# Buffer addresses, a ring's load order and the engine of some splits, changed together in a Strassen MLP kernel

## The chip, the cores and the metric

The kernel runs on one core of a Trainium2 chip. The metric is the device time of one execution in microseconds (us). All inputs, outputs and sums are float32. TensorE (PE) multiplies, VectorE (DVE), ScalarE (ACT) and GpSimd (POOL) work on tiles of 128 partitions in SBUF, and SyncE (SP) issues the DMAs. Each engine takes its instructions in the order of the program.

## The reference

```python
def reference(q, k, v, moe_w_gate, moe_w_val, moe_w_out, moe2_w_in, moe2_w_out):
    x = attention(q, k, v)                  # 4 x 8 heads, 576 positions of 64, causal by blocks of 64
    x = x.transpose(0, 2, 1, 3).reshape(2304, 512)
    g = x @ moe_w_gate                      # 512 -> 1536
    x = (g * sigmoid(g) * (x @ moe_w_val)) @ moe_w_out          # 1536 -> 512
    h = x @ moe2_w_in                       # 512 -> 2048
    g = np.where(h > 0, h, np.exp(np.minimum(h, 0)) - 1)        # ELU
    return g @ moe2_w_out                   # 2048 -> 512
```

## The kernel before

Each float32 factor is split into a high part (rounded to the type in which TensorE multiplies at full pace) and a low part (the rest), and a product is three matmuls: high by high, high by low, low by high (`mm3`, L213 to L215; written out at L1102 to L1104 and L1211 to L1213). ScalarE makes a high part by a copy, another engine the low part by a subtraction.

The stages follow each other: attention, and gate and value products of the first tokens (to about 345 us); gate and value products of the other tokens with one level of Strassen (to 475 us; tiles `xc`, `bt`, `val`, `xa`); the product with `moe_w_out` (to 603 us; tile `y`); then the second MLP. It runs over three groups of 768 tokens (i = 0, 1, 2) and in each over eight pairs p of 128-wide blocks of the 2048 hidden columns. The products of pair p with `moe2_w_in` are seven Strassen products M1 to M7 (`p3_h`; 42 matmuls of 384 columns, tiles `h`, in group 2 also `o`). ELU is made by ScalarE and VectorE (L1052 to L1056) and split into `gp` buffers (high and low, L1056 and L1058), and in groups 0 and 1 the product with `moe2_w_out` follows (`p3_o`: 36 matmuls of 512 columns a pair, tile `o`, 576 matmuls in all; `gp` is the stationary operand, the parts `OH` and `OL` of the weight the moving one). In group 2 that product is Strassen's too (`p3_o7`, after the last pair, 256 columns each, from about 915 us).

The parts that the change touches:

- **Weights of `moe2_w_out`.** `conv_unit` turns each of its 16 blocks (128 x 512) from the raw words into a work tile of a ring of four (`c`), by ScalarE (L188) and VectorE (L196, L198, L200), makes the high part on ScalarE (L206) and the low part on GpSimd (L210). This happens while group 0 runs, between the pairs (603 to 740 us).
- **Combined weights for group 2.** While group 1 runs, `o_sums` adds high and low parts again (L930, one block of a pair on VectorE and one on GpSimd), combines them (L936), splits the results (L946, L947) and stores them to `o_scr`. Its work tiles are four slots of their own (`co`).
- **The ring of weight slots.** The split Strassen weights lie in DRAM (`w_scr`). `p3_slot` (L1004) loads one product's weights into the next of eight slots of the tile `xa`; a slot is free when the product that used it eight slots ago is done. SyncE takes the loads in the order of the ring.
- **Addresses.** `gp` buffers start 16 words (`YO`, 64 bytes) into the tiles `val` and `bt`. By the addresses of the built program, `bt`, `val`, `oh`, `ol` and `xc` start at multiples of 128 bytes, `xa` 64 bytes beyond one.

The order of the instructions on each engine comes from a list scheduler in the kernel (`Plan`): every task has an engine, an assumed duration, a priority (mostly a due time) and its dependencies. So an edit moves the rows around it too.

```python
ns = [p3_slot(p, o, due3[i, p] + step / 7 * u - 8) for u, o in enumerate((M1, M2, M6, M5, M7, M4, M3))]
g = p3_h(i, p, ns, due3[i, p] - (UY + .5 if i == p == 0 else 0), step)
```

Of the kernel before, what the change touches and what calls it, by code (L numbers as in the profile page):

```python
# [150 lines left out]
def attention_moe_moe_kernel(ctx: ExitStack, tc: tile.TileContext,  # L151
# [50 lines left out]
    def like(c, d):  # L202
        return c.rearrange("p (a b) -> p a b", a=2) if len(d.shape) == 3 else c
# [1 line left out]
    def cv_hi(i):  # L205
        act.copy(cv_units[i][1], like(cv_state[i][1], cv_units[i][1]))  # L206

    def cv_lo(i):
        _, hi, lo = cv_units[i]
        pool.tensor_tensor(lo, like(cv_state.pop(i)[1], lo), hi.bitcast(F32), ALU.subtract)  # L210

    def mm3(dst, wh, wl, xh, xl, start, stop, more=False):
        pe.matmul(dst, wh, xh, start=start, stop=False, skip_group_check=more)  # L213
# [47 lines left out]
    def tr_t():  # L261
# [2 lines left out]


    plan = Plan(dict(raw=3, rawb=2, c=4, rk=2, rq=2, rv=NRV, nm=4, sm=3, pl=NP1, ph=NP1, th=NTH, x=3, sa=1, sb=1, tp=2, gv=2,
                     th1=2, s2=2, st=2, ar=5, ah=NAH, gm=KP, co=4, wo=3, e4=4, gs=12, gt=4, y=6, ys=4, ws=NW, wm=NWM, gp=NP, et=2, hc=4, **{f"ab{p}{r}": 1 for p in range(KP) for r in range(4)}))
    add, nxt = plan.add, plan.nxt


# [22 lines left out]
    def conv_unit(i, prio, after=(), whole=False, first=()):  # L293
        cn[i], rn[i] = nxt("c"), nxt("raw" if i < 2 * K1 else "rawb")
        r, c, w = ("raw" if i < 2 * K1 else "rawb", rn[i], 0), ("c", cn[i], 0), ("w", i, 0)
        add("SP", 450, lambda: cv_dma(i), prio, writes=[r], after=first, data=1900 if i == 1 else 1430)
        add("ACT", 575, lambda: cv_a(i), prio, [r], [c])
        for p, ns in enumerate((340, 650, 650) if i < 2 * K1 else (340, 602, 602)):
            if p == 0 and CVP and 4 <= i < 2 * K1 and i % 2 >= 2 - CVP:
                add("POOL", 900, lambda: cv_b(i, 0, pool), prio, [r, c], [c])  # L300
                continue
            add("DVE", ns, lambda p=p: cv_b(i, p), prio, [r, c], [c], data=-1000 if p == 2 and i >= 2 * K1 else 0.0, both=i < 2 * K1)
        if whole:
            return
        add("ACT", 520, lambda: cv_hi(i), prio, [c], [w], after)
        add("POOL", 1250 if i < 2 * K1 else 1400, lambda: cv_lo(i), prio, [c, w], [w])


    heads = lambda t, n: t.rearrange("p (h d) -> p h d", d=n)
# [354 lines left out]
    ar_b, ys_b, abt, pa_t = [], [], [], []  # L664
    OSEQ = M1, M6, M2, M7, M5, M4, M3 = range(7)
    PSEQ = M1, M2, M6, M5, M7, M4, M3
    OH, OL, ws, wm, gp, yqt = {}, {}, {}, {}, {}, {}

    def yq(r):
        return yqt[r].rearrange("p k t -> p (k t)")  # L670
# [247 lines left out]
        strassen_weights(part, ck, whole, prio, split)  # L918

    def o_sums(p, prio):  # L920
        n = [nxt("co") for _ in range(2)]
        part = lambda r, c: pa_t[0][:, 512 * (n[c] % 4) + 256 * r:512 * (n[c] % 4) + 256 * r + 256]
        ck = lambda r, c: ("co", n[c], r)
        plan.group = "o0"
        for x in range(2):
            add("SP", 450, lambda x=x: sp.dma_start(out=o_scr[p][0][:, 256 * x:256 * x + 256], in_=(OH, OL)[x][2 * p][:, 0:256].bitcast(F32)), prio, [("w", unit["o", 2 * p], 0)], [("oscr", p, (M1, x))], data=400)
        for c in range(2):
            def build(c=c):
                f, w = 2 * p + c, pa_t[0][:, 512 * (n[c] % 4):512 * (n[c] % 4) + 512]
                (pool if c else dve).tensor_tensor(w, OH[f].bitcast(F32), OL[f].bitcast(F32), ALU.add)  # L930

            add(*(("POOL", 1400) if c else ("DVE", 690)), build, prio, [("w", unit["o", 2 * p + c], 0)], [ck(0, c), ck(1, c)], [("p3", 0, 0), ("yscr", NG - 1, 2), ("od", (p - 1) % HP, 0)], data=-2000)
        plan.group = None

        def comb(d, x, y, op):
            add("DVE", 420, lambda: dve.tensor_tensor(part(*d), part(*x), part(*y), op), prio, [ck(*x), ck(*y)], [ck(*d)])  # L936

        def split(o, x):
            n = nxt("wo")
            hk, lk = ("wo", n, 0), ("wo", n, 1)  # L940

# [15 lines left out]
        comb(a11, a12, a11, ALU.subtract)  # L957
        split(M3, a11)
# [47 lines left out]
        add("SP", 450, load, prio, [("wscr", p, o)], [("ws", n, 0), ("ws", n, 1)], [("p2", 0, 0)], data=700)  # L1006
        return n

    def p3_h(i, p, ns, due, step):
        q = i * HP + p  # L1010
        m1, u2, u3 = range(3) if i >= S7 else (nxt("hc") for _ in range(3))
        hck = lambda n: ("hc", n, 0)
# [54 lines left out]
        X, Y = q % 2, 1 - q % 2  # L1067
        Z = 2 if three else Y
        for u, (o, b, new) in enumerate(((M1, X, True), (M2, Z, True), (M6, X, False), (M5, Y, True), (M7, X, False), (M4, X, False), (M3, Y, False))):
            for k in range(2):  # L1070
                def mm(u=u, o=o, k=k, b=b, new=new):
                    w, ks, ys = ws[ns[u]], slice(128 * k, 128 * k + 128), slice(HT * k, HT * k + HT)
                    mm3(bank(b), w[:, 0, ks], w[:, 1, ks], yop(o, 0)[:, ys], yop(o, 1)[:, ys], new and k == 0, k == 1, True)

                add("PE", 525, mm, due + u * step / 7 + .01 * k, [("ws", ns[u], 0), ("ws", ns[u], 1), ("yo", o, 0)],
                    [hbk(b)] + ([("hd", i, 0)] if p == HP // 2 and u == 0 and k else [("he", i, 0)] if p == HP - 1 and u == 0 and k else []))
# [50 lines left out]
    def p3_o7(i, due):  # L1127
# [12 lines left out]
        def split(o, p, r, u):  # L1140
            v = nxt("gp")
            hk, lk = ("gp", v, 0), ("gp", v, 1)
            g = lambda k: gp[v % NP][k]
            pr = due - HSTEP * (HP - p) + 10 if u == 0 else by(u, p)
            eng, en, ns = (pool, "POOL", 1100) if u == 0 or p in PLO else (dve, "DVE", 557)
            add("ACT", 412, lambda: act.copy(g(0), gb(p, r)), pr, [gk(p, r)], [hk])
            add(en, ns, lambda: eng.tensor_tensor(g(1), gb(p, r), g(0).bitcast(F32), ALU.subtract), pr, [gk(p, r), hk], [lk])
            return v

# [38 lines left out]
        for u, o in enumerate(seq):  # L1188
# [12 lines left out]
            tail = last and o == M4  # L1201
            for n, (p, j) in enumerate([(p, j) for j in range(3) for p in range(HP)] if tail else [(p, j) for p in range(HP) for j in range(3)]):
                def mm(o=o, p=p, j=j, b=b, new=new, v=vs[p], n=ns.get(p)):
                    h, l = (t[:, 128 * j:128 * j + 128] for t in gp[v % NP])
                    if o in OST:
                        wh, wl = ws[n][:, 0], ws[n][:, 1]
                    else:
                        cs = slice(256 * (o == M4), 256 * (o == M4) + 256)
                        wh, wl = OH[2 * p + 1][:, cs], OL[2 * p + 1][:, cs]
                    d = region(b, (j,))  # L1210
                    pe.matmul(d, h, wh, start=new and p == 0 and j != 1, stop=False, skip_group_check=True)  # L1211
                    pe.matmul(d, h, wl, start=False, stop=False, skip_group_check=True)
                    pe.matmul(d, l, wh, start=False, stop=p == HP - 1, skip_group_check=True)  # L1213
# [385 lines left out]
```

## Time and profile before

| what | value |
|---|---|
| median of 3 runs (lowest, highest) | 982.23 us (982.12, 982.48) |
| the profiled execution | 982.16 us |
| its span in the trace | 980.3 us (1.86 us lie outside) |
| TensorE busy in the span | 965.4 us, 98% |
| VectorE, ScalarE, GpSimd busy | 791.6, 647.7, 244.8 us |
| granted TensorE clock | 1.00, in every slice |

Busy time of TensorE is the union of instructions whose ends are modelled and overlap: a matmul is shown about 0.2 us longer than its distance to the next one. So the pace is read from start to start, and a wait is the extra distance between two starts.

### The profile page before, as it was taken

How to read it: one execution, taken by the hardware profiler on the slowest of the kernel's cores; microseconds unless marked ns; L12 is line 12 of the kernel's file. 1: busy time of each engine (PE TensorE's matmuls, PEld its weight loads, DVE VectorE, ACT ScalarE, POOL GpSimd, SP SyncE). 2: the span in 40 equal slices, each digit the busy share in tenths (PEclk: the TensorE clock that was granted, in tenths of full speed). 3: DMA queues.
4: the chain of work that ended last, by engine and by line, in shares of the span. 5: the costliest groups of instructions: out<-in, count | busy, mean ns of one | idle time of the engine just before them, and what ended most of it. 6: DMA issues, size and time to landing. Idle time of an engine off the chain costs nothing.

```text
span 980.3 us, 18628 instructions
## 1 busy us (share of the span) xinstructions
PE 965.4 (98%) x6266; PEld 871.5 (89%) x6266; DVE 791.6 (81%) x1614; ACT 647.7 (66%) x1521; POOL 244.8 (25%) x243
## 2 busy tenths in 40 slices
PE   9999999999999999999999999999999999999998
PEld 8789988888889978887999999889888888899998
DVE  7999677666867795789999996987977687977993
ACT  6998678888987644556765665665665455666653
POOL 3333442332324623000001101223302323311131
PEclk9999999999999999999999999999999999999999
DMA  6767465566576679774764705787646676596663
GB/s 224 235 201 220 138 193 175 203 214 193 180 247 228 216 262 351 221 254 154 239 194 125 252 17 151 246 275 271 179 123 216 188 240 191 177 295 222 229 208 116
DMA packets 116463, 202.56 MB, mean 207 GB/s; under 512 B 12304, under 2 KB 51216, under 8 KB 116368
## 3 DMA queue, kind: packets, MB, share of 16 engines
q1 hardware_dynamic: 116224, 201.24, 63.5%
q8 instruction: 50, 0.82, 0.4%
q14 instruction: 45, 0.37, 0.1%
q10 hardware_dynamic: 144, 0.13, 0.0%
HBM read 141.56 MB, written 59.77 MB: 205 GB/s over the span
## 4 chain that ended last, share of the span: by engine, by line
PE 86%; DVE 7%; DMA 2%; ACT 2%; issue 1%; POOL 1%; SPq 0%; ACTq 0%; DVEq 0%; POOLq 0%
PE gv L213 7%; PE gv L215 7%; PE gv L214 7%; PE y L213 6%; PE y L214 6%; PE y L215 6%; PE tp L506 5%; PE h L213 4%; PE sa L480 4%; PE h L215 4%; PE h L214 4%; PE o L1104 3%; PE o L1103 3%; PE o L1102 3%; PE tp L601 2%; PE o L1211 2%
## 5 line engine op out<-in xcount | busy, mean ns | idle before, releaser
L213 PE MATMUL gv<-xa,bt 128*128 128x256 f32 x240 | 72.7, 303 | 0.6 <-DVE tt L655 0.6
L213 PE MATMUL gv<-xa,val 128*128 128x256 f32 x240 | 71.9, 300 | 0.0
L213 PE MATMUL h<-val,xa 128*128 128x384 f32 x204 | 69.0, 338 | 0.8 <-ACT xq L1065 0.6
L215 PE MATMUL h<-val,xa 128*128 128x384 f32 x204 | 68.6, 336 | 0.0
L214 PE MATMUL h<-val,xa 128*128 128x384 f32 x204 | 68.4, 335 | 0.0
L606 ACT COPY th<-tp 128x512 f32<-128x512 f32 x96 | 53.7, 593 | 21.7 <-PE tp L602 21.5
L215 PE MATMUL gv<-xa,val 128*128 128x256 f32 x240 | 67.1, 280 | 0.5 <-POOL val L210 0.5
L214 PE MATMUL gv<-xa,bt 128*128 128x256 f32 x240 | 67.0, 279 | 0.0
L215 PE MATMUL gv<-xa,bt 128*128 128x256 f32 x240 | 67.0, 279 | 0.0
L214 PE MATMUL gv<-xa,val 128*128 128x256 f32 x240 | 67.0, 279 | 0.0
L210 POOL TENSOR_TENSOR bt<-c,bt 128x512 fp32r<-128x512 f32 x20 | 30.9, 1547 | 125.7 <-ACT bt L206 65.7
L1313 POOL TENSOR_TENSOR wy<-c,wy 128x256 fp32r<-128x256 f32 x48 | 39.5, 836 | 87.9 <-ACT wy L1312 87.8
L761 ACT ACTIVATE val<-a 128x384 fp32r<-128x384 f32 x80 | 40.8, 524 | 25.3 <-PE y L215 22.7
L915 POOL TENSOR_TENSOR val<-c,val 128x256 fp32r<-128x256 f32 x14 | 12.7, 912 | 174.5 <-ACT val L914 174.4
L506 PE MATMUL tp<-th,rv 128*64 128x256 f32 (+1 forms) x512 | 55.5, 359 | 0.0
L915 POOL TENSOR_TENSOR wy<-c,wy 128x256 fp32r<-128x256 f32 x42 | 32.6, 791 | 86.6 <-ACT wy L914 61.0
L1054 DVE SCALAR_TENSOR_TENSOR xq<-xq,xq 128x384 f32<-128x384 f32 x64 | 38.9, 611 | 14.4 <-ACT xq L1053 14.0
L650 DVE SCALAR_TENSOR_TENSOR tt<-tt,gv 128x256 f32<-128x256 f32 x60 | 25.0, 417 | 31.3 <-ACT tt L646 30.9
L506 PEld LDWEIGHTS tp<-th,rv 128*64 128x64 f32 x512 | 33.9, 136 | 18.2 <-ACT c L188 0.3
L480 PE MATMUL sa<-rk,rq 64*128 64x320 f32 (+2 forms) x192 | 49.9, 393 | 0.0
L480 PE MATMUL sb<-rk,rq 64*128 64x320 f32 (+2 forms) x192 | 49.9, 393 | 0.0
L213 PEld LDWEIGHTS gv<-xa,bt 128*128 128x128 f32 x240 | 45.3, 189 | 4.8 <-issue 2.9
(425 smaller groups left out, 3677.3 us busy)
## 6 DMA issues: line engine op xcount, KB each, us to landing
xa<-w_scr SPq DMA_DIRECT2D x168, 256.0 KB, 3.3
a<-a_scr SPq DMA_DIRECT2D x67, 192.0 KB, 3.5
g_scr<-wy SPq DMA_DIRECT2D x48, 256.0 KB, 2.9
xa<-g_scr SPq DMA_DIRECT2D x48, 256.0 KB, 4.3
w_scr<-wy SPq DMA_DIRECT2D x42, 256.0 KB, 4.4
xa<-o_scr SPq DMA_DIRECT2D x40, 256.0 KB, 3.3
raw<-in_w2i_dram SPq DMA_DIRECT2D x16, 512.0 KB, 4.4
raw<-in_w2o_dram SPq DMA_DIRECT2D x16, 512.0 KB, 4.0
```

Of the source, the lines that this page charges most:

```text
L210: pool.tensor_tensor(lo, like(cv_state.pop(i)[1], lo), hi.bitcast(F32), ALU.subtract)
L213: pe.matmul(dst, wh, xh, start=start, stop=False, skip_group_check=more)
L214: pe.matmul(dst, wh, xl, start=False, stop=False, skip_group_check=more)
L215: pe.matmul(dst, wl, xh, start=False, stop=stop, skip_group_check=more)
L480: pe.matmul(sc[2 * p + j][:, at:at + w], raw["rq"][us, QW * p + 128 * q:QW * p + 128 * q + 128], raw["rk"][us, ext * p + o:ext * p + o + w ...
L506: pe.matmul(st["pv"][64 * j:64 * j + 64, QW * p + o:QW * p + QW], raw["rv"][:, p * (nf + 1) + c, 64 * j:64 * j + 64], x[:, at:at + QW - o] ...
L606: act.copy(out["th", c // 2], st["tr", c])
L761: add("ACT", 412, lambda: act.activation(t(0), ab(p, r, g), ACTF.Copy, scale=0.5), by(u, p), [abk(p, r)], [hk], ([("xcd", o, 0) for o in ( ...
L915: add("POOL", 1000, lambda: pool.tensor_tensor(t()[:, 256:512], part(*x), t()[:, 0:256].bitcast(F32), ALU.subtract), prio, [ck(*x), hk] + ...
L1054: add("DVE", 575, lambda: dve.scalar_tensor_tensor(t(), e(), 1.0, t(), ALU.add, ALU.mult), PMP, [tk, ek], [tk])
L1102: pe.matmul(d, h, OH[f][:, cs], start=(p == 0 and u < 2), stop=False, skip_group_check=True)
L1313: add("POOL", 800, lambda: pool.tensor_tensor(t()[:, 256:512], part(*x), t()[:, 0:256].bitcast(F32), ALU.subtract), prio, [ck(*x), hk] + w ...
```

## The change: what it does

1. `gp` buffers are at offset 0 of their tiles for groups 0 and 1; group 2 uses buffers at the old offset (`gp7`), and the first of its splits wait for the last matmul of `p3_o`.
2. In group 2, from pair 1 on, the slots of the next pair's M1 and M2 are taken between this pair's M7 and M4.
3. `o_sums` takes its work tiles from the ring `c`, builds both sums on VectorE, and waits for `p3_o` of group 0 once instead of pair by pair.
4. The low parts of `moe2_w_out` are made by VectorE.

```diff
-    def cv_lo(i):
+    def cv_lo(i, eng=pool):
         _, hi, lo = cv_units[i]
-        pool.tensor_tensor(lo, like(cv_state.pop(i)[1], lo), hi.bitcast(F32), ALU.subtract)
+        eng.tensor_tensor(lo, like(cv_state.pop(i)[1], lo), hi.bitcast(F32), ALU.subtract)
...
-        add("POOL", 1250 if i < 2 * K1 else 1400, lambda: cv_lo(i), prio, [c, w], [w])
+        if i < unit["o", 0]:
+            add("POOL", 1250 if i < 2 * K1 else 1400, lambda: cv_lo(i), prio, [c, w], [w])
+        else:
+            add("DVE", 690, lambda: cv_lo(i, dve), prio, [c, w], [w])
...
     def o_sums(p, prio):
-        n = [nxt("co") for _ in range(2)]
+        n, full = [nxt("c") for _ in range(2)], {}
...
-                (pool if c else dve).tensor_tensor(w, OH[f].bitcast(F32), OL[f].bitcast(F32), ALU.add)
+                full[c] = w
+                dve.tensor_tensor(w, OH[f].bitcast(F32), OL[f].bitcast(F32), ALU.add)
...
+            if u == 5:
+                if i >= S7 and 0 < p < HP - 1:
+                    need(p + 1, (0, 1))
+                need(p, (5, 6))
+            n = slots[i, p, u]
...
-            g = lambda k: gp[v % NP][k]
+            g, old = (lambda k: gp7[v % NP][k]), [("od", HP - 1, 0)] * (i == S7 and u == 0)
...
-            gp[k] = [vals_t[0][:, YO + 2 * HT * k + HT * x:YO + 2 * HT * k + HT * x + HT] for x in range(2)] if k < 4 else [flat[2 * k + 8 + x][:, YO:YO + HT] for x in range(2)]
+            gp[k], gp7[k] = ([vals_t[0][:, a + 2 * HT * k + HT * x:a + 2 * HT * k + HT * x + HT] for x in range(2)] if k < 4 else [flat[2 * k + 8 + x][:, a:a + HT] for x in range(2)] for a in (0, YO))
...
-            ns = [p3_slot(p, o, due3[i, p] + step / 7 * u - 8) for u, o in enumerate((M1, M2, M6, M5, M7, M4, M3))]
-            g = p3_h(i, p, ns, due3[i, p] - (UY + .5 if i == p == 0 else 0), step)
+            need = lambda x, us, i=i, step=step: [slots.setdefault((i, x, u), p3_slot(x, HSEQ[u], due3[i, x] + step / 7 * u - 8)) for u in us if (i, x, u) not in slots]
+            need(p, range(5 if i >= S7 and p else 7))
+            g = p3_h(i, p, need, due3[i, p] - (UY + .5 if i == p == 0 else 0), step)
```

**The ring's loads.** SyncE's loads for pairs 2 to 7 of group 2, before (`w_scr_85` holds the weights of pair 2, `w_scr_90` of pair 7):

```order
L1004 DMA xa<-w_scr_85 128x512 x3
L1004 DMA xa<-w_scr_86 128x512 x7
L1004 DMA xa<-w_scr_87 128x512 x7
L1004 DMA xa<-w_scr_88 128x512 x7
L1004 DMA xa<-w_scr_89 128x512 x7
L1004 DMA xa<-w_scr_90 128x512 x7
L967 DMA xa<-o_scr_75 128x512
```

The same place after the change:

```order
L1008 DMA xa<-w_scr_86 128x512 x2
L1008 DMA xa<-w_scr_85 128x512 x2
L1008 DMA xa<-w_scr_86 128x512 x3
L1008 DMA xa<-w_scr_87 128x512 x2
L1008 DMA xa<-w_scr_86 128x512 x2
L1008 DMA xa<-w_scr_87 128x512 x3
L1008 DMA xa<-w_scr_88 128x512 x2
L1008 DMA xa<-w_scr_87 128x512 x2
```

Two loads of each next pair now stand ahead of the last two of a pair. TensorE takes the products in such an interleaved order already before.

**The low parts.** GpSimd's rows in group 0 before; `L210` are the low parts of `moe2_w_out`, `L930` a sum of `o_sums`:

```order
L210 TENSOR_TENSOR bt_116<-c,bt_115 128x512
L210 TENSOR_TENSOR ol_7307<-c,oh_7306 128x512
L210 TENSOR_TENSOR bt_118<-c,bt_117 128x512
L210 TENSOR_TENSOR ol_7309<-c,oh_7308 128x512
L210 TENSOR_TENSOR bt_120<-c,bt_119 128x512
L210 TENSOR_TENSOR ol_7311<-c,oh_7310 128x512
L930 TENSOR_TENSOR a<-bt_105,bt_106 128x512
```

None of these stands on GpSimd after the change. VectorE's rows before, at the end of that stretch (about 697 to 706 us; L1061 adds a product to a kept one and frees the PSUM bank for which TensorE waits):

```order
L198 SCALAR_TENSOR_TENSOR c<-raw_101,c 128x512
L1061 TENSOR_TENSOR xq_140<-h_5993,xq_140 128x384
L200 SCALAR_TENSOR_TENSOR c<-raw_101,c 128x512
L849 TENSOR_TENSOR raw_101<-tt,raw_100 128x768
L1054 SCALAR_TENSOR_TENSOR xq_142<-xq_143,xq_142 128x384
L1055 SCALAR_TENSOR_TENSOR xq_142<-xq_142,xq_140 128x384
L1054 SCALAR_TENSOR_TENSOR xq_142<-xq_143,xq_142 128x384
L1061 TENSOR_TENSOR xq_141<-h_5993,xq_141 128x384
```

VectorE's rows after, at the same place (L1061 is now L1067, L1054 and L1055 are L1060 and L1061, L849 is L852):

```order
L210 TENSOR_TENSOR bt_120<-c,bt_119 128x512
L1067 TENSOR_TENSOR xq_140<-h_5993,xq_140 128x384
L196 TENSOR_SCALAR c<-c 128x512
L198 SCALAR_TENSOR_TENSOR c<-raw_101,c 128x512
L200 SCALAR_TENSOR_TENSOR c<-raw_101,c 128x512
L1060 SCALAR_TENSOR_TENSOR xq_142<-xq_143,xq_142 128x384
L1067 TENSOR_TENSOR xq_141<-h_5993,xq_141 128x384
L1061 SCALAR_TENSOR_TENSOR xq_142<-xq_142,xq_140 128x384
L1060 SCALAR_TENSOR_TENSOR xq_142<-xq_143,xq_142 128x384
L210 TENSOR_TENSOR ol_7311<-c,oh_7310 128x512
```

The low parts stand between ELU and the conversions, and the combination of L849 comes later than the addition (L1067) that frees the bank.

## Rows read from the trace of the kernel before

**Rows 1.** Page, part 1, TensorE: busy time, share of the span, instructions.

```profile
PE 965.4 (98%) x6266; PEld 871.5 (89%) x6266; DVE 791.6 (81%) x1614; ACT 647.7 (66%) x1521; POOL 244.8 (25%) x243
```

**Rows 2.** Windows by stage: length, busy time (count) of each engine, clock, DMA.

```profile
475.00:603.00 128.00, 128.00 (x740) 128.00 (x739) 117.77 (x236) 77.64 (x159) 6.39 (x7) 1.00 0.46 151
603.00:740.00 137.00, 133.88 (x665) 118.95 (x664) 118.60 (x199) 86.92 (x182) 33.55 (x24) 1.00 0.71 222
740.00:862.00 122.00, 121.84 (x606) 108.86 (x605) 95.56 (x165) 68.11 (x153) 38.57 (x39) 1.00 0.64 203
862.00:916.00 54.00, 51.36 (x287) 49.00 (x287) 41.90 (x77) 36.35 (x82) 6.93 (x7) 1.00 0.78 252
```

**Rows 3.** TensorE's waits, whole span: us in total, times, longest.

```profile
PE h L213 <- DVE xq L1061: 2.5, 2, 1.5
PE h L213 <- DMA xa<-w_scr: 2.4, 3, 1.3
```

**Rows 4.** TensorE's timeline in group 1: start, shown length, instruction.

```profile
762.20 0.39 PE L1102 MATMUL o<-bt,bt 128*128 128x512 f32 x1
...
763.60 0.34 PE L213 MATMUL h<-val,xa 128*128 128x384 f32 x1
```

**Rows 5.** TensorE's timeline in the Strassen gate stage, 512 columns.

```profile
385.68 0.39 PE L213 MATMUL y<-xc,xa 128*128 128x512 f32 x1
...
388.42 0.39 PE L213 MATMUL gv<-xc,bt 128*128 128x512 f32 x1
...
391.14 0.39 PE L213 MATMUL y<-val,xa 128*128 128x512 f32 x1
```

**Rows 6.** TensorE's timeline in group 2 [idle before, and what ended it].

```profile
874.93 0.34 PE L215 MATMUL o<-val,xa 128*128 128x384 f32 x1
876.01 0.41 PE L213 MATMUL h<-wy,xa 128*128 128x384 f32 x1 [0.74 <-DMA xa<-w_scr]
...
892.36 0.41 PE L213 MATMUL h<-wy,xa 128*128 128x384 f32 x1 [1.32 <-DMA xa<-w_scr]
```

**Rows 7.** Chain that ended last, in order of time, group 2: start, us, what.

```profile
903.93 3.81 DMA xa<-w_scr
...
911.80 3.70 DMA xa<-o_scr
```

**Rows 8.** VectorE's groups of instructions, 600 to 740 us: busy us, mean ns.

```profile
L1054 DVE SCALAR_TENSOR_TENSOR xq<-xq,xq 128x384 f32<-128x384 f32 x36 | 22.4, 623 | 7.7 <-ACT xq L1053 7.4
L1055 DVE SCALAR_TENSOR_TENSOR xq<-xq,xq 128x384 f32<-128x384 f32 x27 | 16.8, 621 | 0.3
L1058 DVE TENSOR_TENSOR val<-xq,val 128x384 fp32r<-128x384 f32 x19 | 14.8, 777 | 2.7 <-ACT val L1056 2.7
L198 DVE SCALAR_TENSOR_TENSOR c<-raw,c 128x512 int32<-128x512 int32 x16 | 13.0, 817 | 0.2
```

**Rows 9.** Lines L1054 and L930, whole span: duration ns min/median/max.

```profile
L1054 DVE SCALAR_TENSOR_TENSOR xq<-xq,xq x64: 541/557/1648, 601.9 to 851.7; 128x384 f32<-128x384 f32 x64
L930 DVE TENSOR_TENSOR a<-oh,ol x6: 678/678/1320, 769.0 to 852.2; 128x512 f32<-128x512 f32 x6
```

**Rows 10.** Chain that ended last, before TensorE's two waits for L1061.

```profile
651.33 1.67 DVE c L200
...
654.06 1.57 DVE xq L1054
...
702.04 1.54 DVE xq L1055
703.59 1.55 DVE xq L1054
```

**Rows 11.** GpSimd's timeline at the same places.

```profile
650.70 1.75 POOL L210 TENSOR_TENSOR bt<-c,bt 128x512 fp32r<-128x512 f32 x1 [3.64 <-DMA w_scr<-val]
...
701.51 1.66 POOL L210 TENSOR_TENSOR ol<-c,oh 128x512 fp32r<-128x512 f32 x1 [3.51 <-ACT oh L206]
703.13 1.59 POOL L930 TENSOR_TENSOR a<-bt,bt 128x512 f32<-128x512 f32 x1
```

More of the change, by code (lines that the diff above doesn't have):

```diff
@@ L266, in attention_moe_moe_kernel @@
     plan = Plan(dict(raw=3, rawb=2, c=4, rk=2, rq=2, rv=NRV, nm=4, sm=3, pl=NP1, ph=NP1, th=NTH, x=3, sa=1, sb=1, tp=2, gv=2,
-                     th1=2, s2=2, st=2, ar=5, ah=NAH, gm=KP, co=4, wo=3, e4=4, gs=12, gt=4, y=6, ys=4, ws=NW, wm=NWM, gp=NP, et=2, hc=4, **{f"ab{p}{r}": 1 for p in range(KP) for r in range(4)}))
+                     th1=2, s2=2, st=2, ar=5, ah=NAH, gm=KP, wo=3, e4=4, gs=12, gt=4, y=6, ys=4, ws=NW, wm=NWM, gp=NP, et=2, hc=4, **{f"ab{p}{r}": 1 for p in range(KP) for r in range(4)}))
     add, nxt = plan.add, plan.nxt
@@ L666, in attention_moe_moe_kernel @@
     PSEQ = M1, M2, M6, M5, M7, M4, M3
-    OH, OL, ws, wm, gp, yqt = {}, {}, {}, {}, {}, {}
+    OH, OL, ws, wm, gp, gp7, yqt = {}, {}, {}, {}, {}, {}, {}
     def yq(r):
@@ L920, in o_sums @@
     def o_sums(p, prio):
-        n = [nxt("co") for _ in range(2)]
-        part = lambda r, c: pa_t[0][:, 512 * (n[c] % 4) + 256 * r:512 * (n[c] % 4) + 256 * r + 256]
-        ck = lambda r, c: ("co", n[c], r)
+        n, full = [nxt("c") for _ in range(2)], {}
+        part = lambda r, c: full[c][:, 256 * r:256 * r + 256]
+        ck = lambda r, c: ("c", n[c], r)
         plan.group = "o0"
@@ L928, in build @@
             def build(c=c):
-                f, w = 2 * p + c, pa_t[0][:, 512 * (n[c] % 4):512 * (n[c] % 4) + 512]
-                (pool if c else dve).tensor_tensor(w, OH[f].bitcast(F32), OL[f].bitcast(F32), ALU.add)
-            add(*(("POOL", 1400) if c else ("DVE", 690)), build, prio, [("w", unit["o", 2 * p + c], 0)], [ck(0, c), ck(1, c)], [("p3", 0, 0), ("yscr", NG - 1, 2), ("od", (p - 1) % HP, 0)], data=-2000)
+                f, w = 2 * p + c, conv.tile([128, 512], F32, tag="c", name="c", bufs=4)
+                full[c] = w
+                dve.tensor_tensor(w, OH[f].bitcast(F32), OL[f].bitcast(F32), ALU.add)
+            add("DVE", 690, build, prio, [("w", unit["o", 2 * p + c], 0)], [ck(0, c), ck(1, c)], [("p3", 0, 0), ("yscr", NG - 1, 2), *([("od", HP - 1, 0)] if p == 0 else [])], data=-2000)
         plan.group = None
@@ L1007, in p3_slot, with p3_h @@
         return n
-    def p3_h(i, p, ns, due, step):
+    HSEQ, slots = (M1, M2, M6, M5, M7, M4, M3), {}
+    def p3_h(i, p, need, due, step):
         q = i * HP + p
@@ L1069, in p3_h, with mm @@
         for u, (o, b, new) in enumerate(((M1, X, True), (M2, Z, True), (M6, X, False), (M5, Y, True), (M7, X, False), (M4, X, False), (M3, Y, False))):
+            if u == 5:
[3 more added lines that the diff above has]
+            n = slots[i, p, u]
             for k in range(2):
-                def mm(u=u, o=o, k=k, b=b, new=new):
-                    w, ks, ys = ws[ns[u]], slice(128 * k, 128 * k + 128), slice(HT * k, HT * k + HT)
+                def mm(n=n, o=o, k=k, b=b, new=new):
+                    w, ks, ys = ws[n], slice(128 * k, 128 * k + 128), slice(HT * k, HT * k + HT)
                     mm3(bank(b), w[:, 0, ks], w[:, 1, ks], yop(o, 0)[:, ys], yop(o, 1)[:, ys], new and k == 0, k == 1, True)
-                add("PE", 525, mm, due + u * step / 7 + .01 * k, [("ws", ns[u], 0), ("ws", ns[u], 1), ("yo", o, 0)],
+                add("PE", 525, mm, due + u * step / 7 + .01 * k, [("ws", n, 0), ("ws", n, 1), ("yo", o, 0)],
                     [hbk(b)] + ([("hd", i, 0)] if p == HP // 2 and u == 0 and k else [("he", i, 0)] if p == HP - 1 and u == 0 and k else []))
@@ L1142, in split @@
             hk, lk = ("gp", v, 0), ("gp", v, 1)
-            g = lambda k: gp[v % NP][k]
+            g, old = (lambda k: gp7[v % NP][k]), [("od", HP - 1, 0)] * (i == S7 and u == 0)
             pr = due - HSTEP * (HP - p) + 10 if u == 0 else by(u, p)
             eng, en, ns = (pool, "POOL", 1100) if u == 0 or p in PLO else (dve, "DVE", 557)
-            add("ACT", 412, lambda: act.copy(g(0), gb(p, r)), pr, [gk(p, r)], [hk])
+            add("ACT", 412, lambda: act.copy(g(0), gb(p, r)), pr, [gk(p, r)], [hk], old)
             add(en, ns, lambda: eng.tensor_tensor(g(1), gb(p, r), g(0).bitcast(F32), ALU.subtract), pr, [gk(p, r), hk], [lk])
@@ L1203, in mm @@
                 def mm(o=o, p=p, j=j, b=b, new=new, v=vs[p], n=ns.get(p)):
-                    h, l = (t[:, 128 * j:128 * j + 128] for t in gp[v % NP])
+                    h, l = (t[:, 128 * j:128 * j + 128] for t in gp7[v % NP])
                     if o in OST:
```

## Prediction

> **What bounds the kernel now.** I read the page first: TensorE is busy for 965.4 us, 98% of the span [rows 1]. So nothing that only lightens another engine can be worth more than the 15 us in which TensorE stands still, and a larger gain has to come out of the pace of its matmuls. Next the windows by stage [rows 2]: from 475 to 603 us TensorE shows no idle time, from 603 to 740 us 3.1 us (133.88 of 137), from 740 to 862 us 0.2 us, from 862 to 916 us 2.6 us. The change moves no instruction before 603 us, so these late stretches are where it can act. Who ends the waits there is in TensorE's waits [rows 3]: twice VectorE (L1061, 2.5 us in total), three times the load of a weight slot (2.4 us). Last I took the pace from TensorE's timeline, start to start, since the shown lengths overlap: six matmuls of 512 columns in group 1 take from 762.20 to 763.60 us, 233 ns each [rows 4]. In the gate stage twelve matmuls of the same width take from 388.42 to 391.14 us, 226.7 ns each [rows 5]. The reader is to see that equal matmuls run at two paces, and that both kinds of wait stand at known places.
>
> **The change part by part.**
>
> *Addresses.* In the faster run of [rows 5] both operands (`xc` or `val` moving, `bt` or `val` stationary) start at multiples of 128 bytes. In [rows 4] the moving weights do, but the stationary `gp` starts 64 bytes beyond. The change puts `gp` at offset 0 for groups 0 and 1, so the 576 matmuls of `p3_o` become like the faster run: 233.3 - 226.7 = 6.6 ns each, 3.8 us if all gain it. The run before the faster one in [rows 5], mostly with `xa` (64 bytes beyond) as the stationary operand, takes 2.74 us for twelve, 228.3 ns; a gain that ends there is 5.0 ns each, 2.9 us. I take 3.2 us: about one `p3_o` matmul in six is followed by a matmul of `p3_h`, whose weights keep their place, and no row shows that neighbour, so I count 5/6 of 3.8. Nothing excludes no gain at all, so the term runs from 0 to 3.8 us; a loss has no row that suggests it, since no run with equal starts is slower than one with unequal ones.
> [...]
>
> *Ring order.* In group 2 TensorE takes products in an order other than that of the ring, so some slots are reloaded late. At 874.93 us the last matmul before a wait starts, the next at 876.01: 1.08 us where matmuls follow each other every 0.173 us (740 in 128 us, rows 2), so 0.91 us are lost, 0.17 us more than the 0.74 us that are shown as idle [rows 6]. With three waits of 2.4 us idle in all [rows 3] that makes 2.4 + 3 x 0.17 = 2.9 us. The third of them is 2.4 - 0.74 - 1.32 = 0.34 us. A fourth load, the first of `o_scr`, also lies on the chain, 3.70 us long [rows 7]; I count it like the third, 0.34 us. Together 3.3 us. Does the new order remove them? By the program's order, between the last use of the slot and its next need lie 15 matmuls at 876 and at 892 us, 2.6 us, against a landing of up to 3.81 us [rows 7]. After the change the shortest such distances are 24 (4.2 us, the first slot of `p3_o7`) and 27 matmuls (4.7 us), others are about 7 us. 4.2 us is only 0.4 us above the landing, so I keep the bounds at 2.4 and 3.7 us (a second short one counted) and take 3.3. The loads of M4 and M3 now queue on SyncE behind two loads of the next pair. They wait longer for their slots, and TensorE waits for them if that costs more than the 0.9 us between 4.7 and 3.8.
>
> *Low parts on VectorE.* VectorE gets 16 subtractions of 128 x 512. It shows a sum of that size at 678 ns in the median [rows 9]: 10.9 us in a stretch in which it is busy for 118.6 of 137 us [rows 2]. GpSimd loses 16 of its 24 instructions there, 1.6 to 1.75 us each [rows 11], about 26 of its 33.6 us. Those slowed VectorE: L1054 takes 557 ns in the median of the run [rows 9] but 623 in this stretch, which over 36 makes 2.4 us; L1055 with 621 over 27 makes 1.7, L1058 with 777 over 19 makes 4.2, L198 with 817 against about 680 over 16 makes 2.2 us [rows 8]. These four groups alone hold 10.5 us, of which the low parts' share (26 of 33.6) is 8.1 us. So VectorE's total hardly moves (10.9 against 8.1 or a little more), and what counts is where the long instructions fall. Both waits of TensorE for L1061 end chains with two of them: 1.67 and 1.57 us before 656 us, 1.54 and 1.55 us before 706 us [rows 10]. GpSimd's low parts lie beside them, once a sum of `o_sums`, L930 [rows 11]. Without GpSimd the first chain is 1.67 + 1.57 - 0.68 - 0.56 = 2.0 us shorter, with two low parts in it 1.36 us longer, 0.64 net of a wait of about 1.0. The second is 2.0 us shorter as well, with one low part (0.68) longer, and L849 stands behind the needed addition now: 1.3 us of the wait of 1.5. That is 1.9 us, and 0.1 for the restart of the matmul after a wait (0.17 us each, as above, in part): 2.0 us. Bounds: 2.8 us if both waits go (2.5 + 2 x 0.17), and a loss of 10.9 us if VectorE gets nothing back and every subtraction ends on the path.
> [...]
>
> *What I cost at nothing.* The sums of `o_sums`: eight more of 678 ns on VectorE (5.4 us) from 740 us on, where it is busy for 95.6 of 122 us and TensorE idles for 0.2 [rows 2]. The eight of GpSimd that go had slowed VectorE too (1.55 us at 703.59). Without that cover they cost 5.4 us. The ring `c` for their work tiles: a build waits until the tile four places earlier is split, behind it on VectorE stand ELU and its low parts, for which `p3_o` waits. One GpSimd instruction of 1.6 us is the most that it waits for at a time, and a pair of group 1 lasts some 15 us. The wait of the first `gp7` splits for the end of `p3_o`: they are needed at the first load of `o_scr`, 911.8 us [rows 7], some 50 us later.
>
> **Sum.** 3.2 + 3.3 + 2.0 = 8.5 us off the profiled execution's 982.16 us: 973.7 us. The median of the three runs is 982.23, 0.07 us above it, so I don't correct for that.
>
> **The rivals.**
>
> *The start address sets nothing.* The pace of `p3_o` could come from its alternation with `p3_h`, not from `gp`. For it: matmuls of 384 columns run at 0.173 us in the stage from 475 us, with equal starts [rows 2], and, with a moving operand 64 bytes off, in group 2 as well (after the wait in rows 6), so the start is not felt everywhere. Against it: 228.3 against 226.7 ns in one stage [rows 5]. 982.16 - 3.3 - 2.0 = 976.9 us. [...] By the rows 13 in 100.
>
> *VectorE gives nothing back on the path.* The low parts fall into the same chains, and the waits stay or move. For it: 118.6 of 137 us busy [rows 2], and VectorE's order is fixed, so a subtraction that waits for ScalarE's high part holds up ELU. Against it: rows 10 and 11. 982.16 - 3.2 - 3.3 = 975.7 us; 15 in 100.
>
> *The ring's waits come back as waits for a bank.* With the loads in time, TensorE goes faster through group 2, and the next to be late are the additions on VectorE (41.9 of 54 us busy, rows 2) that free PSUM banks. If half of the 3.3 us returns: 975.4 us; 11 in 100.
>
> *Slower: VectorE becomes the bound from 603 to 740 us.* If the long instructions had another cause than the low parts, VectorE would have 118.6 + 10.9 = 129.5 us of work in 137, in an order without gaps, and TensorE would wait for L1067. It decides against the change once more than 3.2 + 3.3 = 6.5 of the 10.9 us end on the path. With all of them 982.16 - 6.5 + 10.9 = 986.6 us. Rows 10 and 11 speak against it. 6 in 100.
>
> **How the numbers follow.** The three terms as summed have 55 in 100. The range reaches down to all upper bounds and one small wait more (3.8 + 3.7 + 2.8 + 1.3 = 11.6 us: 970.6, taken as 970.5), and up to two terms failing at once (3.5 us or so left: 978.6). That leaves out the slower case and some mishaps, under 2 in 10. A measurement of this kernel tells about 0.2% (2 us) from no change. All cases but the last lie more than 2 us below 982.2, so faster has 0.90, leaving 0.04 for within 0.2% and 0.06 for slower.
>
> **What the new profile would show.** Addresses: runs of `p3_o` matmuls at 227 ns from start to start; 233 would refute the term. Ring: no wait of TensorE for `xa<-w_scr` or `xa<-o_scr` in group 2 and fewer than 1 us idle between 862 and 916 us; a wait for L1038's successor (L1044) in its place is the third rival. Low parts: no L210 on GpSimd after 603 us, L1060 (before: L1054) back at 560 ns in the mean of 600 to 740 us, VectorE's busy time there about as before, and TensorE's waits for L1067 under 1 us in total. The prediction is wrong if TensorE's idle time from 603 to 740 us grows beyond 4 us, or if a matmul of 512 columns does not get faster.

## The result, and the profile after

The changed kernel takes 973.68 us (median of 5 runs, 973.21 to 975.17), the kernel before 982.48 us (5 runs, 982.12 to 984.61). The ratio is 0.9907, with a 95% interval from 0.9893 to 0.9921. The forecast was 973.7 us.

The page, part 1, and the windows of the stages, columns as in [rows 1, 2]:

```profile
PE 962.0 (99%) x6266; PEld 872.8 (90%) x6266; DVE 791.3 (81%) x1637; ACT 646.4 (66%) x1521; POOL 209.2 (21%) x220
```
```profile
603.00:740.00 137.00, 135.86 (x685) 122.60 (x684) 118.14 (x219) 88.93 (x187) 7.12 (x8) 1.00 0.71 228
740.00:862.00 122.00, 122.00 (x617) 110.51 (x616) 98.77 (x176) 70.56 (x158) 29.61 (x33) 1.00 0.68 209
862.00:916.00 54.00, 53.38 (x322) 53.03 (x322) 44.92 (x81) 37.21 (x87) 7.59 (x8) 1.00 0.79 256
```

TensorE's idle time falls from 3.1 to 1.1 us in group 0 and from 2.6 to 0.6 us in group 2. VectorE does 20 instructions more from 603 to 740 us in the same busy time (118.60 before, 118.14 now), while GpSimd's falls from 33.55 to 7.12 us. TensorE's waits from 600 us on, to compare with [rows 3], are two kinds:

```profile
PE h L213 <- ACT xq L1071: 1.1, 2, 0.6
PE o L213 <- DMA xa<-w_scr: 0.6, 1, 0.6
```

The waits for VectorE are gone, and those for a slot are one instead of three. A wait for ScalarE's copy of a bank (L1071, before L1065) was there once at 605 us and is there twice now, at 607 and 613 us. VectorE's groups from 600 to 740 us, beside [rows 8]:

```profile
L1060 DVE SCALAR_TENSOR_TENSOR xq<-xq,xq 128x384 f32<-128x384 f32 x36 | 19.9, 554 | 6.6 <-ACT xq L1059 6.3
L1061 DVE SCALAR_TENSOR_TENSOR xq<-xq,xq 128x384 f32<-128x384 f32 x27 | 15.6, 576 | 0.2
...
L1064 DVE TENSOR_TENSOR val<-xq,val 128x384 fp32r<-128x384 f32 x20 | 11.8, 591 | 1.7 <-ACT val L1062 1.6
...
L198 DVE SCALAR_TENSOR_TENSOR c<-raw,c 128x512 int32<-128x512 int32 x16 | 11.0, 686 | 0.1
```

The same instructions took 623, 621, 777 and 817 ns. So VectorE took on the low parts and got about as much back on these instructions; experiment 4 tests that it was GpSimd that had slowed them.

**How kernels are compared below.** The five runs of the changed kernel lie 2 us apart, those of other kernels here up to 9 us, and some of that comes before anything was changed. The profiled execution of the changed kernel, 975.17 us, is the longest of its five. Two matmuls stand at the same place of TensorE's order in all kernels: the one that waits for L1065 or L1071, between 605 and 610 us, and the last. Between them lies the first matmul of group 2. Starts before and after, from TensorE's timeline:

```profile
605.24 0.45 PE L213 MATMUL h<-val,xa 128*128 128x384 f32 x1 [0.57 <-ACT xq L1065]
...
862.46 0.44 PE L213 MATMUL h<-wy,xa 128*128 128x384 f32 x1
...
976.94 0.28 PE L1213 MATMUL o<-bt,bt 128*128 128x256 f32 x1
```
```profile
607.14 0.45 PE L213 MATMUL h<-val,xa 128*128 128x384 f32 x1 [0.57 <-ACT xq L1071]
...
858.86 0.34 PE L213 MATMUL h<-wy,xa 128*128 128x384 f32 x1
...
969.96 0.28 PE L1224 MATMUL o<-bt,bt 128*128 128x256 f32 x1
```

The changed kernel comes 1.9 us later to the first of them. From there on it is 371.70 - 362.82 = 8.9 us shorter, which agrees with the medians (8.8). Of this, 257.22 - 251.72 = 5.5 us lie in groups 0 and 1, and 114.48 - 111.10 = 3.4 us in the rest (group 2 and its output). All kernels, read in the same way (us):

```
kernel                                    groups 0,1   rest   together  median   ratio to before (95%)
before                                      257.22    114.48   371.70
changed                                     251.72    111.10   362.82   973.68   0.9907 (0.9893-0.9921)
before + ring order          (b_ring)       256.90    109.28   366.18   979.12   0.9951 (0.9932-0.9970)
before + low parts on DVE    (b_lo)         254.11    114.36   368.47   978.89   0.9957 (0.9944-0.9971)
before + o_sums              (b_sums)       255.21    113.17   368.38   979.65   0.9961 (0.9945-0.9977)
changed, gp at 64 bytes      (a_addr64)     254.03    110.76   364.79   975.34   0.9917 (0.9892-0.9943)
changed, old ring order      (a_noring)     251.71    113.01   364.72   975.90   0.9927 (0.9910-0.9944)
changed, low parts on POOL   (a_lopool)     255.95    110.22   366.17   976.32   0.9931 (0.9913-0.9949)
changed, old o_sums          (a_nosums)     251.86    112.71   364.57   975.25   0.9908 (0.9894-0.9922)
changed, GpSimd beside DVE   (a_pooldup)    254.36    110.87   365.23   975.99   0.9917 (0.9895-0.9938)
changed, M2 ahead of M1      (a_swap)       251.71    110.24   361.95   973.24   0.9899 (0.9885-0.9912)
changed, gp7 at 0            (a_gp7_0)      251.71    112.09   363.80   974.75   0.9913 (0.9896-0.9930)
changed, gp at 32 / 32       (a_32_32)      254.26    110.50   364.76   976.37   0.9929 (0.9917-0.9942)
changed, gp at 16 / 48       (a_16_48)      253.95    110.77   364.72   975.53   0.9924 (0.9911-0.9938)
```

Groups 0 and 1 repeat within 0.02 us where the order and the buffers are the same (changed, a_noring, a_swap, a_gp7_0). The rest does not, since DMA landings set some of it: from 110.2 to 111.1 us in the four kernels with TensorE's order and buffers of the changed one there (changed, a_addr64, a_lopool, a_pooldup), in which TensorE waits for a load for 0.6, 0.3, 0 and 0.2 us. The intervals of the ratios from a_addr64 on all overlap with that of the changed kernel. So what is said of these kernels rests on the trace, of one execution each.

### The profile page after: what moved, and what is told of

Read it like the earlier page. It is cut to its first block, busy times and chain, and to the rows that moved or that the text cites. A ratio compares the mean times of both kernels' runs of the same rounds, so it can differ in the third digit from the quotient of the medians.

```text
span 973.4 us, 18625 instructions
## 1 busy us (share of the span) xinstructions
PE 962.0 (99%) x6266; PEld 872.8 (90%) x6266; DVE 791.3 (81%) x1637; ACT 646.4 (66%) x1521; POOL 209.2 (21%) x220
## 4 chain that ended last, share of the span: by engine, by line
PE 86%; DVE 8%; ACT 2%; DMA 2%; issue 1%; SPq 0%; POOL 0%; DVEq 0%; ACTq 0%
PE gv L213 7%; PE gv L215 7%; PE gv L214 7%; PE tp L509 5%; PE h L213 5%; PE h L215 5%; PE h L214 5%; PE o L1115 5%; PE o L1113 5%; PE o L1114 5%; PE sa L483 4%; PE y L214 4%; PE y L213 4%; PE y L215 4%; PE tp L604 2%; PE o L1222 2%
## 5 line engine op out<-in xcount | busy, mean ns | idle before, releaser
L951 POOL TENSOR_TENSOR a<-c,a 128x256 fp32r<-128x256 f32 x22 | 19.1, 874 | 154.7 <-ACT a L950 154.7
L213 PEld LDWEIGHTS gv<-xa,val 128*128 128x128 f32 x240 | 45.3, 189 | 2.3 <-issue 2.3
```

## The experiments

**1. The addresses** (a_addr64). Every engine's order stays that of the changed kernel.

```diff
-            gp[k], gp7[k] = (... for a in (0, YO))
+            gp[k], gp7[k] = (... for a in (YO, YO))
```

> The changed kernel with gp back at 64 bytes for groups 0 and 1, every engine's order as in the changed kernel. The profile of the changed kernel shows p3_o at 229 ns from start to start where the kernel before had 233. If the start address sets the pace: the p3_o matmuls go back to about 233 ns and the time rises by 576 x 3.6 ns = 2.1 us or up to the 3.2 us of the forecast, to 975.8 to 976.9 us. If the address sets nothing (the pace of the changed kernel comes from its other order, or from GpSimd's absence): p3_o stays at 229 ns and the time at 973.7 us.

Twelve `p3_o` matmuls in a row in group 1, of the changed kernel and then of this one, start, shown length, instruction:

```profile
764.25 0.39 PE L1113 MATMUL o<-oh,bt 128*128 128x512 f32 x1
...
766.77 0.39 PE L1115 MATMUL o<-oh,val 128*128 128x512 f32 x1
```
```profile
763.87 0.40 PE L1113 MATMUL o<-oh,bt 128*128 128x512 f32 x1
...
766.44 0.39 PE L1115 MATMUL o<-oh,val 128*128 128x512 f32 x1
```

Eleven steps take 2.52 us (229.1 ns each) and 2.57 us (233.6 ns). Over all `p3_o` matmuls, gaps over 245 ns left out, the mean is 229.3 ns after, 232.9 here and 232.7 before. Groups 0 and 1 are 2.3 us longer, and the time (975.34 us) lies 0.5 us under the range that was expected for this case. The address sets the pace, and the rival of the start address that sets nothing falls. The order of the work has no part in it: at 64 bytes the pace is the same in the order of before.

**2. Each other part alone** (on the kernel before). The edits are the hunks of the diff for the ring, for `cv_lo`, and for `o_sums`.

> The kernel before with the new ring order alone. By the forecast's theory the DMA waits at 876, 892, 908 and 915 us go and nothing takes their place: 982.4 - 3.3 = 979.1 us, and the windows from 862 to 916 us show under 1 us of idle TensorE. By the rival in which half returns as waits for a PSUM bank: 980.8 us, with waits for L1044's place in the profile. If the landings and not the order made those waits: about 982.4 us.

> The kernel before with the low parts of moe2_w_out on VectorE alone; the sums of o_sums stay half on GpSimd. By the forecast's theory (GpSimd's long subtractions slow VectorE, and the two waits of 656 and 706 us hang on that): 982.4 - 2.0 = 980.4 us, at best 2.8 us off (979.6). The wait at 706 us has one instruction slowed by an L930 sum of GpSimd, which stays, so up to 0.9 us of it may stay. If VectorE becomes the bound: up to 993 us. If the waits went in the changed kernel because of the moved sums and conversions and not because of GpSimd: 982.4 us or somewhat more.

> The kernel before with o_sums' tiles from the ring c and both sums on VectorE alone; low parts stay on GpSimd. By the forecast it costs and gives nothing (982.4 us, within 1 us). Rival: the sums' 5.4 us on VectorE were hidden only because the low parts' part of the change gave VectorE time back, and alone they lengthen the waits from 603 to 740 us: 983 to 985 us. Other rival: the GpSimd sum at 703 us was one of the two slow places of the 706 us wait, and without it that wait shortens by up to 0.9 us: 981.5 us.

The ring order alone takes 114.48 - 109.28 = 5.2 us off the rest, of which 1.2 us come from another thing (last section) and 4.0 from the waits; TensorE's list of waits from 860 us on is empty, and the time is the one expected. The low parts alone take 3.1 us off groups 0 and 1, more than the 2.8 us that were expected at best: no wait for VectorE is left there. The sums alone take 2.0 us off the same place, where the forecast had nothing: the wait at 656 us stays, the one at 706 us is 1.1 us shorter, and two small ones at 640 and 801 us (0.34 and 0.43 us with the matmul behind them) are gone. The edit takes GpSimd's sums at 703 us [rows 11] and at 798 us away; why the wait at 640 us goes, with no sum near it, stays open. The gains can't be added, 3.1 + 2.0 is more than the 5.5 - 2.3 = 3.2 us that groups 0 and 1 gain beside the addresses.

**3. Each part undone** in the changed kernel.

> The changed kernel with the low parts of moe2_w_out back on GpSimd; addresses, ring order and o_sums as changed. By the forecast's theory the wait at 656 us (1.25 us with the restart) comes back whole, that at 706 us in part: 1.3 to 2.5 us more, 975.0 to 976.2 us. If moving the sums (which alone took away more than half of the 706 us wait) is what took the waits away: 973.7 us. If the low parts cost VectorE more than they give: under 973.2 us.

> The changed kernel with the old ring order of group 2. By the forecast's theory the DMA waits of group 2 come back: 3.3 us more, 977.0 us; by the profile of the ring order alone, in which group 2 was 4.3 us shorter, 978.0 us. If the waits were the landings' and not the order's: 973.7 us.

> The changed kernel with o_sums as before (work tiles of its own, one sum of a block pair on GpSimd). By the forecast the sums are worth nothing: 973.7 us. If the GpSimd sums lengthen a wait that the low parts don't reach (706 us, or the waits in group 2), up to 1 us more: 974.7 us. If the eight sums on VectorE cost something on the path: up to 1 us less, 972.7 us.

With the low parts on GpSimd, the chain of waits into TensorE's longest wait, and GpSimd's timeline beside it:

```profile
656.03 1.68 DVE c L200
...
658.76 1.54 DVE xq L1057
```
```profile
655.66 1.49 POOL L210 TENSOR_TENSOR bt<-c,bt 128x512 fp32r<-128x512 f32 x1 [3.38 <-ACT bt L206]
658.43 1.46 POOL L210 TENSOR_TENSOR ol<-c,oh 128x512 fp32r<-128x512 f32 x1 [1.28 <-ACT oh L206]
```

GpSimd's two instructions end at 657.15 and 659.89 us. VectorE's two, begun while they ran, end 0.56 and 0.41 us later: most of the 0.68 and 0.56 us that they take elsewhere (medians of L200 and L1054 in the kernel before) comes after GpSimd is done. Behind the wait TensorE ran at half pace in this execution. The window (columns as in [rows 2]):

```profile
660.80:664.60 3.80, 3.77 (x11) 3.39 (x12) 2.83 (x6) 2.97 (x7) 0.00 (x0) 0.55 0.69 217
```

Six matmuls of 384 columns lose 0.146 us each and five of 512 lose 0.197, together 1.9 us. Without that groups 0 and 1 are 255.95 - 251.72 - 1.9 = 2.4 us longer. So the low parts are needed, also where the sums have moved. This edit moves rows of the other engines as well and does not tell GpSimd from their order; experiment 4 does.

The old ring order costs 1.9 us in the rest, less than the 3.3 us that were expected and more than nothing. TensorE's waits there, from 860 us on:

```profile
PE h L213 <- DVE xq L1037: 0.6, 1, 0.6
PE o L1215 <- DMA xa<-o_scr: 0.4, 1, 0.4
PE o L213 <- DMA xa<-w_scr: 0.4, 1, 0.4
PE h L213 <- DMA xa<-w_scr: 0.3, 1, 0.3
```

Two of the three DMA waits are at the places of before (907.87 and 915.54 us there), and the other one is at a matmul that did not wait there. At the place of the first (876.01 us) VectorE came last in this execution, and the one of 892.36 us is gone. So which load is late differs between these executions. The old sums cost 0.14 us in groups 0 and 1: once the low parts have left GpSimd, theirs don't matter. The 1.6 us in the rest are one late landing and the first of `o_scr`, and the ratio is that of the changed kernel; I give the sums nothing for it.

**4. What it is in GpSimd** (a_pooldup). One instruction more beside each low part on VectorE. It subtracts the high part (`cv_units[i][1]`) from itself, and its result is never read (shortened at each `...`):

```diff
-            add("DVE", 690, lambda: cv_lo(i, dve), prio, [c, w], [w])
+            add("DVE", 690, lambda: cv_lo(i, dve), prio, [c, w], [w]); add("POOL", 1400, lambda: pool.tensor_tensor(pa_t[0][:, 1536:2048], *[... for t in cv_units[i][1:2] * 2], ALU.subtract), prio, [w], [], [...])
```

> The changed kernel with one more GpSimd subtraction of 128 x 512 beside each of the 16 low parts that VectorE makes: it reads the same high part twice and writes to a place that nothing reads. The order of TensorE, VectorE, ScalarE and SyncE is that of the changed kernel, so nothing waits for the added work; it only runs at the same time. If GpSimd's long subtractions by themselves slow VectorE: L1060 goes from 554 ns back to 600 or more in the mean of 600 to 740 us, VectorE's busy time there from 118 to 124 us or more, and TensorE's waits for VectorE come back, by 2.4 us (what putting the low parts back on GpSimd cost) up to 8 us: 976.1 to 981.7 us. If the waits went because of the other order of VectorE's instructions: 973.7 us, L1060 at 554 ns.

The window from 603 to 740 us, three groups of VectorE's (behind them two of these groups in the changed kernel) and TensorE's waits:

```profile
603.00:740.00 137.00, 134.28 (x671) 119.69 (x670) 126.73 (x216) 86.58 (x182) 30.59 (x23) 1.00 0.73 225
```
```profile
L1061 DVE SCALAR_TENSOR_TENSOR xq<-xq,xq 128x384 f32<-128x384 f32 x27 | 18.7, 691 | 0.2
L1067 DVE TENSOR_TENSOR xq<-h,xq 128x384 f32<-128x384 f32 x27 | 14.9, 551 | 3.9 <-PE h L215 2.7 <-ACT xq L1071 0.9 <-ACT val L917 0.2
...
L210 DVE TENSOR_TENSOR ol<-c,oh 128x512 fp32r<-128x512 f32 x6 | 6.7, 1116 | 0.2 <-ACT oh L206 0.2
```
```profile
L1067 DVE TENSOR_TENSOR xq<-h,xq 128x384 f32<-128x384 f32 x27 | 15.0, 554 | 9.0 <-PE h L215 6.0 <-ACT xq L1071 2.9
...
L210 DVE TENSOR_TENSOR ol<-c,oh 128x512 fp32r<-128x512 f32 x6 | 4.1, 686 | 0.2 <-ACT oh L206 0.2
```
```profile
PE h L213 <- ACT xq L1071: 1.5, 2, 0.9
PE h L213 <- DVE xq L1067: 1.1, 2, 0.9
```

With 30.59 - 7.12 = 23.5 us more on GpSimd, VectorE is busy for 8.6 us more (with 216 instructions in the window instead of 219), and groups 0 and 1 are 2.6 us longer. The low parts themselves are hit most, since the added work becomes ready together with them: those of `ol` go from 686 to 1116 ns. L1061 goes from 576 to 691 ns. L1060 goes only from 554 to 570 ns, not to the 600 that were expected, while [rows 8] have it (L1054 there) at 623: which instruction is hit differs between the kernels. L1067, which has one of its two inputs in PSUM, stays as it was (554 and 551 ns). No order of TensorE, VectorE or ScalarE changed and nothing waits for the added work, so running beside VectorE is what costs. That the low parts of the kernel before cost in the same way, on other instructions, is the reading of [rows 8, 10, 11] that this supports. Of the 23.5 us that GpSimd runs longer, 8.6 show in VectorE's busy time; no run here shows what sets that share.

**5. The ring's last short distances** (a_swap). The wait that is left in the changed kernel, from its chain of waits:

```profile
873.09 5.23 DMA xa<-w_scr
878.32 0.04 issue
878.36 0.45 PE o L213
```

Between two users of that slot stand 27 matmuls, 4.7 us. The edit loads the next pair's M2 first, since TensorE takes half of it first; that makes 33 matmuls, 5.7 us:

```diff
-                    need(p + 1, (0, 1))
+                    need(p + 1, (1, 0))
```

> The changed kernel with the next pair's M2 ahead of its M1 in the ring (M2's first three matmuls are taken ahead of the slots of this pair's M7 and the next M1). The changed kernel and three others with its ring order show DMA waits of TensorE at the same four places, where 27 matmuls (4.7 us) or fewer lie between two users of a slot: 0.2 to 2.2 us in all, in the mean some 0.9 us. With the swap these distances are 33 matmuls (5.7 us), the first of p3_o7 27. If the distance decides: group 2 shows no DMA wait before its last slot, and takes 48.9 us (as it did where none was) instead of 49.8; the time is 972.8 us or up to 0.5 us more. If the loads are late for want of DMA throughput, waits of the same sum appear elsewhere in group 2: 973.7 us.

TensorE waits for no DMA from 600 us on, and the rest takes 110.24 us instead of 111.10. That is what was expected if the distance decides, but it does not show it. The three other kernels that show no such wait, a_lopool, a_32_32 and b_ring, have the next pair's M1 first, and the rest of a_lopool takes 110.22 us. So with the distance of 27 matmuls some executions wait and some don't, and one execution without a wait can be chance. By the ratios the swap is not told apart from the changed kernel either (0.9899 and 0.9907, intervals that overlap). It has the lowest median of all kernels that were run.

**6. What the start address does** (a_gp7_0, a_32_32, a_16_48). Only the two numbers of `for a in (0, YO)` change, to (0, 0), (8, 8) and (4, 12) words; every order stays.

> The changed kernel with the gp buffers of group 2 at offset 0 too, every engine's order as in the changed kernel. If the start of the stationary operand sets the pace of every matmul: the 504 of p3_o7 (256 columns) go from 117.5 ns to between 112 and 115 ns, 1.3 to 2.8 us less: 970.9 to 972.4 us. If it matters for 512 columns alone, or if p3_o7's pace comes from what else reads SBUF then (the kernel before with the new ring order ran them at 115 ns from the same addresses): 973.7 us.

> The changed kernel with gp at 32 bytes in all groups, every engine's order as in the changed kernel. p3_o ran at 229.3 ns with gp at 0 and 232.9 at 64 bytes; p3_o7 at 120.0 ns at 0 and 117.8 at 64. If only a multiple of 64 bytes counts (a 32-byte start is like neither or is worse): p3_o over 233 ns, over 2 us more. If the pace goes smoothly with the distance between the two operands' starts: p3_o about 231 and p3_o7 about 119 ns, 1.0 + 0.6 us more: 975.3 us. If a page of 64 bytes is what counts, 32 is like 0: p3_o 229.3, p3_o7 120.0: 974.8 us.

> The changed kernel with gp of groups 0 and 1 at 16 bytes and of group 2 at 48, every engine's order as in the changed kernel. If the pace goes smoothly with the start: p3_o about 230.2 ns and p3_o7 about 118.3 ns, 0.5 + 0.3 us more: 974.5 us. If a block of 64 bytes is what counts, both are like 0: p3_o 229.3, p3_o7 120.0 ns: 974.8 us. If any start off a multiple of 64 bytes costs: p3_o over 233 ns, p3_o7 over 120 ns, over 3 us more: 977 us or more.

Mean step from start to start, by the start of `gp` beyond a multiple of 128 bytes; the moving operand is always at a multiple:

```
start of gp, bytes             0       16      32      48      64
p3_o, 512 columns, ns        229.3   232.1   232.5     -     232.9
p3_o7, 256 columns, ns       120.0     -     118.3   117.8   117.8
```

Only 0 stands out, and the other way for 256 columns: `p3_o7` loses 2.2 ns a matmul there, 1.1 us over 504, and the time is 974.75 us, over both values that were expected for it. Twenty of its steps in the kernel with `gp7` at 0, and twenty in the changed one:

```profile
940.00 0.28 PE L1223 MATMUL o<-xa,val 128*128 128x256 f32 x1
...
942.40 0.28 PE L1222 MATMUL o<-xa,val 128*128 128x256 f32 x1
```
```profile
936.16 0.28 PE L1222 MATMUL o<-xa,val 128*128 128x256 f32 x1
...
938.52 0.28 PE L1224 MATMUL o<-xa,val 128*128 128x256 f32 x1
```

None of the three expectations that were written for 16 and 32 bytes (smooth, by blocks of 64, worse than 64) is met.

## Why the prediction was right, by its steps

**Addresses, 3.2 us: right in kind, 2.3 measured.** The step that failed is the pace that the matmuls were to reach. They were to "become like the faster run", 226.7 ns; they came to 229.3, 3.4 ns less than the mean before instead of 6.6. That is 2.0 of the 2.3 us; the other 0.3 are steps of 384 columns beside them and small waits. The row borrowed from another stage gave the sign and not the size. In the gate stage itself, with `xa` as the stationary operand (64 bytes beyond), the mean step is 229.0 ns, and with `bt` or `val` 227.2 ns (285 and 207 steps of the kernel before, gaps over 245 ns left out): the two kinds differ by 1.8 ns there, so most of the 6.6 ns lay between the stages. The deduction to 5/6 was not needed: the matmuls of `p3_o` that a matmul of `p3_h` follows went from 232.7 to 229.6 ns. The reason given against a loss, that no run with equal starts is slower than one with unequal ones, held for the rows shown and not for this kernel: `p3_o7` with equal starts is slower (120.0 ns against 117.8). The stage from 475 us does not have equal starts throughout, as the first rival says (`xa` is the moving operand of a third of its matmuls), but both kinds take 173 or 174 ns there in most steps.

**Ring order, 3.3 us: 3.4 measured in the whole, 4.0 alone, 1.9 undone.** The waits go, as forecast, and don't come back as waits for a bank: that rival has no row in group 2. The margin was thinner than "the 0.9 us between 4.7 and 3.8": the landing behind the wait that is left took 5.23 us, and in the kernel with the old sums 5.40 us. That the three figures differ is the landings' doing: against the 110.24 us without DMA waits, the old order costs 4.2 us in the execution of before, 2.8 in a_noring, and the new order still 0.9 in the changed kernel.

**Low parts on VectorE, 2.0 us: about 3.2 measured together with the sums, 3.1 alone, 2.4 undone.** The term was sized too low, and its upper bound of 2.8 us too. I had counted the waits at 656 and 706 us; the smaller ones at 640 and 801 us went as well, 0.34 and 0.43 us from start to start. Against that stands the second wait for ScalarE at 613 us, 0.8 us with its restart, which no step named. That VectorE gets back as much as it takes on was right: the four groups of [rows 8] went back to 554 to 686 ns, and its busy time did not move. That VectorE gives nothing back on the path, and that it becomes the bound, fall with it; a_pooldup shows what the latter looks like when GpSimd's work stays: 126.73 us busy of 137.

**The sums, nothing: right in the whole, by luck of the overlap.** Undone they change groups 0 and 1 by 0.14 us. Alone they give 2.0; 1.1 of it is at 706 us, where they take GpSimd from one of the two places on which the wait hung. The forecast had that instruction in its rows and put its whole gain down to the low parts.

**The sum.** 8.5 us forecast, 8.9 by the trace, 8.8 by the medians. It came out because the addresses' 0.9 us too much and the low parts' 1.2 us too little met. That is luck; the right total is no proof of the terms.

**The announced signs.** As announced, TensorE is idle for under 1 us from 862 to 916 us (0.6) and for under 4 us in group 0 (1.1), it waits for L1067 for under 1 us (not at all), L1060 is at 560 ns (554), and VectorE's busy time is as before. No L210 was to stand on GpSimd after 603 us: of `moe2_w_out` there is none, of another weight one, at 605.60 us. Runs of `p3_o` were to be at 227 ns, with 233 to refute the term: they lie between. No wait for `xa<-w_scr` was to be left: there is one.

## What to carry to other kernels

When a fully busy engine sets the time, look at the distance between its starts in equal instructions, and try the buffer's start; but measure each shape, since the same move helped 512 columns here (232.9 to 229.3 ns) and hurt 256 (117.8 to 120.0). Work that left GpSimd cost VectorE nothing here (118.60 us busy before, 118.14 with 20 instructions more): compare the means of VectorE's instructions beside GpSimd's with those apart before adding up busy times. A ring of slots can be too short where the order of its loads and the order of their use differ (here three waits, 2.4 us in all); count the user's instructions between two users of a slot, and set them against the longest landing (5.6 us in group 2 of the kernel before), not the usual one (3.8 us in the median there).

## What the runs showed that I had not expected

**One pace or another from the same addresses.** In the kernel with the ring order alone, `p3_o7` goes at 117.8 ns up to a step of 0.19 us instead of 0.12 at 938.46 us, and at 113.3 ns from then to its end, with the addresses and the sequence of the matmuls the same as before. Steps ahead of it and behind it:

```profile
937.33 0.28 PE L1218 MATMUL o<-xa,bt 128*128 128x256 f32 x1
...
938.15 0.28 PE L1219 MATMUL o<-xa,bt 128*128 128x256 f32 x1
938.27 0.35 PE L1220 MATMUL o<-xa,bt 128*128 128x256 f32 x1
938.46 0.28 PE L1218 MATMUL o<-xa,bt 128*128 128x256 f32 x1
...
948.00 0.28 PE L1218 MATMUL o<-xa,val 128*128 128x256 f32 x1
...
950.60 0.28 PE L1220 MATMUL o<-xa,val 128*128 128x256 f32 x1
```

Seven steps in 0.82 us ahead, 23 in 2.60 us behind. This gives the 1.2 us named in experiment 2. A hesitation of 0.06 us at the same matmul in the kernel with the old sums did not do it (117.8 ns behind it). So the pace depends on more than the addresses (117.8 and 113.3 ns with the same ones); what else it depends on was not tried and stays open.

**Half clock behind a wait.** In one execution (a_lopool) a wait of 1.8 us was followed by 3.8 us at a granted clock of 0.55 in the mean, with matmuls of 384 columns at 0.32 us a step instead of 0.17 and of 512 at 0.43 instead of 0.23. That cost 1.9 us, as much again as the wait. The same execution shows a second such stretch, 43.2 to 46.7 us at 0.51 in the mean, 2 us behind a wait of 1.4 us. Behind the waits of up to 1.5 us in [rows 3] the clock stayed at 1.00. So the length of a wait alone does not tell whether the clock falls; what does was not tried.
